# The four half-empty blocks of P turned with 66 columns and copied as 64 partitions; the program's order written as a table of places

## The chip, the cores and the metric

One core of one Trainium2 chip runs the kernel. The metric is device time in microseconds (us) of one execution: 604.06 us before, the median of three runs (603.72 to 604.91). A smaller number is better. The engines are named as in the profile: PE multiplies matrices, PEld is its weight load, DVE, ACT and POOL work on elements, and SP issues most transfers.

## What is computed

Causal attention (batch 4, 12 heads, 448 tokens, head size 64) followed by a two-layer network with squared ReLU (1792 tokens, width 768, hidden width 2048), all in fp32:

```python
attn = softmax(where(causal, q @ k.T / 8, -1e9))        # q, k, v: 4 x 12 x 448 x 64
x = (attn @ v).transpose(0, 2, 1, 3).reshape(1792, 768)
h = maximum(x @ w_in, 0)                                # w_in 768 x 2048
out = (h * h) @ w_out                                   # w_out 2048 x 768
```

## The kernel before

The 48 heads are handled as 24 **pairs** of heads, each in one of two sets of buffers, whose names begin with a or b. In a pair a **chunk** c (0 to 6) is 64 queries of both heads, so 128 partitions. By the causal mask chunk c sees 64(c+1) keys. The steps of a pair are:

- q and k are loaded and turned, on DVE (L403), or for six pairs as rows of 112 tokens on PE (L389).
- PE forms the scores of the chunks (L422). DVE masks each chunk and takes its extreme (L435), ACT takes the exponential and the row sum (L439).
- DVE adds 1e-9 to the seven sums and inverts them (L515, L516). Each chunk of P is then scaled by its inverse, on POOL (L448) or on DVE (L450).
- P is cut into 16 **blocks** (c, kc) of 128 rows by 128 keys, and PE turns them in four **quads** of four (L462). A block is the weight operand, and the identity moves past it. Each quad fills one PSUM bank, and one copy of 128x512 takes it to pt, on ACT (L318) or DVE (L470).
- When all of pt is there, PE multiplies it by v (L482). ACT and DVE split the result into two fp32r halves.

Four blocks, (0,0), (2,1), (4,2) and (6,3), are **half-empty**: only 64 of their 128 keys lie inside the mask. The other half of P was set to zero once, at the start, and is turned like the rest. Before, the list of blocks runs by kc, so the half-empty ones are spread over the quads.

The network's products are made in fp32r as sums of three products (L679 to L681, L1098 to L1100 in the first half). The other half uses a scheme with seven products instead of eight for 2x2 blocks (L860 to L864, L986 to L988). Between these stand the splitting of the weights, loaded as words (L640, L643, L321, L325), and the squares g (L321 on DVE, L325 on POOL).

Every step is an op of a `Plan`. An op has a rank, what it depends on, the buffers that it takes, and one or more ways, each an engine with a cost. Before, `emit` simulated the engines with these costs and took at each step the op that could start first, ties by rank; a table of some hundred amendments shifted ranks. The order that comes out is the order of the instructions in every engine's queue, and each engine works through its queue strictly in that order. The tiles of PSUM (eight banks, `ps`) are handed out in the same pass.

Of the kernel before, what the change touches and what calls it, by code (L numbers as in the profile page):

```python
# [20 lines left out]
class Op:  # L21
    __slots__ = ("rank", "ways", "then", "left", "ready", "take", "drop", "lag", "bias")
# [14 lines left out]
class Plan:  # L37

    LAG = {PE: 0.25, ACT: 0.3, DVE: 0.3, POOL: 0.3, DMA: 0.5, DMA2: 0.5}
    ISSUE = 1.4
    BEGIN, BACKLOG = 1.3, 2.5
    FEW = {PE: 0.0, ACT: 0.5, DVE: 1.0, POOL: 0.0, DMA: 0.0, DMA2: 0.0}
    MANY = {PE: 0.0, ACT: 0.0, DVE: 0.3, POOL: 0.0, DMA: 0.0, DMA2: 0.0}

    def __init__(self):  # L50
        self.ops, self.writer, self.readers = [], {}, {}
        self.pools, self.caps, self.held = {}, {}, {}
        self.bias = self.FEW

# [17 lines left out]
    def op(self, rank, ways, reads=(), writes=(), after=(), take=None, drop=(), clear=(), lag=0.0):  # L72
        o = Op()
        o.rank, o.ways, o.then, o.ready, o.take, o.drop = rank, ways, [], 0.0, take, drop
        o.lag, o.bias = lag, self.bias
# [18 lines left out]
        o.left = len(deps)  # L94
        for d in deps:
            d.then.append(o)
# [3 lines left out]
    def amend(self, table):  # L100
        for first, end, more in table:
            for o in self.ops[first:end]:
                o.rank += more

    def emit(self):
        free = [1.0, 1.9, 3.4, 2.7, 0.7, 0.7]
        ready = [o for o in self.ops if o.left == 0]
        order, port, net = [], 0.0, 0.0
        while ready:
            best = None  # L110
            for o in ready:
                at = o.ready + (self.ISSUE if o.ways[0][0] >= DMA else 0.0)
                if o.take:
                    h, n = o.take[0], len(o.take)
                    if self.held[h.kind] + n > self.caps[h.kind] or len(self.pools[h.pool]) < n:
                        continue
                    at = max(at, sorted(self.pools[h.pool])[n - 1][0])
                at += o.lag
                if o.ways[0][0] >= DMA:
                    at = max(at, net - self.BACKLOG)  # L120

                w = min(
                    (max(free[w[0]], at, port if shared(w) else 0.0) + w[1] + o.bias[w[0]],
                     max(free[w[0]], at, port if shared(w) else 0.0), i, w[0])
                    for i, w in enumerate(o.ways)
                )
                key = (w[1], o.rank)
                if best is None or key < best[0]:
                    best = (key, o, w)
            _, o, (_, start, i, e) = best  # L130
            ready.remove(o)
            free[e] = end = start + o.ways[i][1]
            if shared(o.ways[i]):
                port = max(port, end)
            if e >= DMA:
                net = max(net, start + self.BEGIN) + o.ways[i][3]
                end = max(end, net)
            order.append((start, len(order), o, i))
            for h in o.take:
                entry = min(self.pools[h.pool])  # L140
                self.pools[h.pool].remove(entry)
                h.tile = entry[1:]
                self.held[h.kind] += 1
            for h in o.drop:
                h.drops -= 1
                h.free = max(h.free, end + self.LAG[e])
                if h.drops == 0:
                    self.pools[h.pool].append((h.free,) + h.tile)
                    self.held[h.kind] -= 1
            for t in o.then:  # L150
                same = all(x[0] == e for x in t.ways) and e < DMA
                t.ready = max(t.ready, end + (0.0 if same else self.LAG[e]))
                t.left -= 1
                if t.left == 0:
                    ready.append(t)
        assert len(order) == len(self.ops)
        order.sort(key=lambda x: x[:2])
        for _, _, o, i in order:
            o.ways[i][2]()
        return max(free)  # L160
# [30 lines left out]
def kernel(  # L191
# [47 lines left out]
    TOFF = [P * next(i for i, t in enumerate(TURNED) if t[1] == kc) for kc in range(NK)]  # L239
    NV = 3  # L240
# [10 lines left out]
    class Buffers:  # L251
        def __init__(s, nm, pool):
# [91 lines left out]
    def attention(s, n, at):  # L344
# [109 lines left out]
        def transposed_p(i, at):  # L454

            ps = Hold("ps", "pt")
            blocks = TURNED[4 * i:4 * i + 4]

            def go():
                for n, (c, kc) in enumerate(blocks):  # L460
                    o = QC * (PLACE[c][0] & 1)
                    nc.tensor.transpose(  # L462
                        ps.t[:, n * P:(n + 1) * P],
                        s.p[:, POFF[c] + kc * P:POFF[c] + (kc + 1) * P], ident[:, o:o + P])
            plan.op(at, [(PE, 4 * 0.109, go)], [(nm, "p", c) for c, _ in blocks], [ps],
                    take=ps, clear=[(nm, "pt", i)], lag=spare(1.6))
            t = s.pt[:, 4 * i * P:4 * (i + 1) * P]
            plan.op(at, [
                on_act(512, lambda: t, lambda: ps.t, True),
                (DVE, t_dve(512) + 0.05, lambda: nc.vector.tensor_copy(t, ps.t)),  # L470
            ], [ps], [(nm, "pt", i)], drop=[ps])

        def times_v(av, at):
# [3 lines left out]
            def go():  # L477
                for kc in range(NK):
# [8 lines left out]
                    [(vr, kc) for kc in range(NK)] + [(nm, "pt", i) for i in range(len(TURNED) // 4)], [av], take=av, drop=[vr],  # L487
# [35 lines left out]
        for i in range(len(TURNED) // 4):  # L523
            transposed_p(i, at)
# [675 lines left out]
    plan.bias = plan.MANY  # L1200
# [8 lines left out]
    for gr, u in stages:  # L1209
# [7 lines left out]
    AMENDS = (  # L1217
# [83 lines left out]
```

## Time and profile before

| | before |
|---|---|
| median of three runs | 604.06 us |
| the profiled execution | 606.17 us, of which its span is 604.3 us |
| TensorE's granted clock, mean | 0.999 of full speed |
| PE busy | 587.0 us, 97% of the span |
| weight loads (PEld) | 513.8 us, 85% |
| DVE / ACT / POOL busy | 418.8 / 361.8 / 348.1 us (69 / 60 / 58%) |

Busy time says in which share of the span an engine had something running. The wait view says for whom an engine stood idle. The timeline gives starts, from which the distance between successive instructions is read; a matmul's own duration includes its way through the array, so the distance, not the duration, is what one more of them costs.

### The profile page before, as it was taken

The numbers are of one execution on the slowest core, as the hardware profiler recorded it, in microseconds if no ns is written. First come the engines' busy times: TensorE is split into PE (matmuls) and PEld (weight loads), VectorE is DVE, ScalarE is ACT, GpSimd is POOL, SyncE is SP. The second block draws the span as 40 slices with busy tenths as digits, with TensorE's granted clock in tenths as the row PEclk, the third lists the DMA queues.
The fourth block names the chain that finished last, engine by engine and source line by source line (L and its number), as shares of the span: only waits on it lengthen the run. The fifth ranks groups of instructions, "written<-read, shape, count | busy, mean of one in ns | idle before, by whom it ended". The sixth has DMA issues, their size and how long they took to land.

```text
span 604.3 us, 11456 instructions
## 1 busy us (share of the span) xinstructions
PE 587.0 (97%) x3766; PEld 513.8 (85%) x3766; DVE 418.8 (69%) x951; ACT 361.8 (60%) x889; POOL 348.1 (58%) x460
## 2 busy tenths in 40 slices
PE   3999999999999999999999999999999999999997
PEld 2677777898988998888898889998999899999996
DVE  4997976366985887775677616688782777777454
ACT  3889997665687656577447543367764573752400
POOL 2574673764585844867557754256685566777000
PEclk9999999999999999999999999999999999999999
DMA  9899745979789888987898759869868746771555
GB/s 148 168 204 179 165 103 116 257 232 329 191 208 315 247 238 217 282 232 226 255 242 259 268 189 263 274 188 238 207 152 163 195 116 135 158 177 41 183 92 93
DMA packets 190652, 120.02 MB, mean 199 GB/s; under 512 B 126016, under 2 KB 178560, under 8 KB 190592
## 3 DMA queue, kind: packets, MB, share of 16 engines
q1 hardware_dynamic: 169488, 107.99, 64.8%
q0 software_dynamic: 6912, 9.44, 10.0%
q10 hardware_dynamic: 14192, 1.85, 1.9%
q8 instruction: 30, 0.49, 0.3%
q14 instruction: 30, 0.25, 0.2%
HBM read 80.71 MB, written 38.54 MB: 197 GB/s over the span
## 4 chain that ended last, share of the span: by engine, by line
PE 90%; DMA 4%; ACT 2%; SPq 2%; issue 1%; DVE 0%; ACTq 0%; DVEq 0%
PE ps L1098 7%; PE ps L679 7%; PE ps L1100 6%; PE ps L1099 6%; PE ps L681 6%; PE ps L680 6%; PE ps L482 6%; PE ps L462 6%; PE ps L986 6%; PE ps L988 6%; PE ps L987 6%; PE ps L422 5%; PE ps L860 5%; PE ps L864 5%; PE ps L862 5%; DMA words<-in_moe_w_in_dram 2%
## 5 line engine op out<-in xcount | busy, mean ns | idle before, releaser
L318 ACT ACTIVATE words<-words 128x384 f32<-128x384 f32 (+3 forms) x140 | 79.8, 597 | 27.9 <-DVE words L321 15.3
L448 POOL TENSOR_SCALAR ap<-ap,asm 128x64 f32<-128x64 f32 (+6 forms) x123 | 74.6, 626 | 30.6 <-DVE asm L516 27.7
L435 DVE CUSTOM_DVE_ANT_0 ps<-ps,mask 128x448 f32<-128x448 f32 (+6 forms) x168 | 68.4, 446 | 19.2 <-PE ps L422 12.9
L1098 PE MATMUL ps<-wo,g 128*128 128x384 f32 x224 | 76.8, 343 | 0.0
L1100 PE MATMUL ps<-wo,g 128*128 128x384 f32 x224 | 75.1, 335 | 0.0
L1099 PE MATMUL ps<-wo,g 128*128 128x384 f32 x224 | 75.0, 335 | 0.0
L679 PE MATMUL ps<-x,wi 128*128 128x448 f32 x192 | 74.1, 386 | 0.6 <-ACT aqt L318 0.6
L681 PE MATMUL ps<-x,wi 128*128 128x448 f32 x192 | 70.3, 366 | 0.0
L680 PE MATMUL ps<-x,wi 128*128 128x448 f32 x192 | 70.3, 366 | 0.0
L439 ACT ACTIVATE ap<-ps,mx 128x448 f32<-128x448 f32 (+6 forms) x126 | 59.2, 487 | 15.0 <-DVE mx L435 11.1
L325 POOL TENSOR_TENSOR wi<-words,wi 128x384 fp32r<-128x384 f32 (+1 forms) x44 | 52.6, 1204 | 11.8 <-ACT wi L318 6.6
L860 PE MATMUL ps<-x,wi 128*128 128x448 f32 x156 | 57.3, 367 | 0.3 <-DMA wi<-wi_split 0.3
L318 ACT ACTIVATE r<-ps 128x448 f32<-128x448 f32 x60 | 32.5, 545 | 41.4 <-PE ps L681 17.5
L862 PE MATMUL ps<-x,wi 128*128 128x448 f32 x156 | 57.2, 367 | 0.0
L864 PE MATMUL ps<-x,wi 128*128 128x448 f32 x156 | 57.2, 367 | 0.0
L986 PE MATMUL ps<-g,wi 128*128 128x448 f32 x153 | 56.0, 366 | 0.3 <-DMA wi<-wo_split 0.3
L987 PE MATMUL ps<-g,wi 128*128 128x448 f32 x153 | 56.0, 366 | 0.0
L988 PE MATMUL ps<-g,wi 128*128 128x448 f32 x153 | 56.0, 366 | 0.0
L331 POOL TENSOR_SCALAR wi<-words 128x384 fp32r<-128x384 f32 (+1 forms) x39 | 26.9, 689 | 46.6 <-DVE words L643 23.0
L640 DVE TENSOR_SCALAR words<-words 128x384 int32<-128x384 int32 (+1 forms) x56 | 30.3, 543 | 23.2 <-ACT words L318 23.1
L321 DVE CUSTOM_DVE_ANT_0 words<-words 128x768 uint16<-128x768 uint16 (+1 forms) x56 | 42.3, 755 | 5.8 <-ACT words L318 3.3
L318 ACT ACTIVATE apt<-ps 128x512 f32<-128x512 f32 x65 | 35.6, 611 | 14.5 <-PE ps L462 14.4
(149 smaller groups left out, 1459.9 us busy)
## 6 DMA issues: line engine op xcount, KB each, us to landing
words<-in_moe_w_in_dram SPq DMA_DIRECT2D x24, 512.0 KB, 5.6
words<-in_moe_w_out_dram SPq DMA_DIRECT2D x32, 384.0 KB, 3.7
wo_split<-wo SPq DMA_DIRECT2D x26, 384.0 KB, 4.8
wi<-wo_split SPq DMA_DIRECT2D x24, 384.0 KB, 4.1
wo_whole<-words SPq DMA_DIRECT2D x32, 192.0 KB, 3.9
wi_split<-wi SPq DMA_DIRECT2D x24, 256.0 KB, 4.0
v<-in_v_dram SPq DMA_DIRECT2D x24, 192.0 KB, 4.1
wi_whole<-words SPq DMA_DIRECT2D x18, 256.0 KB, 4.0
```

What stands on the lines that cost most here:

```text
L318: return (ACT, t_act(n, psum, more), lambda: nc.scalar.activation(dst(), src(), func, **kw))
L679: nc.tensor.matmul(o, w[:, 0], x[:, 0], start=c == 0, stop=False)
L680: nc.tensor.matmul(o, w[:, 0], x[:, 1], start=False, stop=False)
L681: nc.tensor.matmul(o, w[:, 1], x[:, 0], start=False, stop=c == NP - 1)
L860: nc.tensor.matmul(o, w.t[:, 0, c], x[:, 0], start=begin and c == 0, stop=False, skip_group_check=True)
L862: nc.tensor.matmul(o, w.t[:, 0, c], x[:, 1], start=False, stop=False, skip_group_check=True)
L986: nc.tensor.matmul(o, w.t[:, 0, d], g.t[:, 0], start=start, stop=False, skip_group_check=True)
L987: nc.tensor.matmul(o, w.t[:, 0, d], g.t[:, 1], start=False, stop=False, skip_group_check=True)
L988: nc.tensor.matmul(o, w.t[:, 1, d], g.t[:, 0], start=False, stop=stop, skip_group_check=True)
L1098: nc.tensor.matmul(res(), g[:, 0], w[:, 0], start=f == 0, stop=False)
L1099: nc.tensor.matmul(res(), g[:, 0], w[:, 1], start=False, stop=False)
L1100: nc.tensor.matmul(res(), g[:, 1], w[:, 0], start=False, stop=f == GF - 1)
```

## The change

The list `QUADS` names the quads by hand. Three have four full blocks each, and the last one collects the four half-empty blocks. In it the weight operand is 66 columns wide (`SLIM`) instead of 128, so the result has 66 partitions instead of 128; the identity that moves keeps its 128 columns. Of the result 64 partitions are copied to pt, in two copies of 64 partitions by 2x128 that wait for the same PSUM bank. The lower 64 partitions of these blocks of pt are set to zero at the start, and of P only two columns per half-empty block. A full quad's copy is one instruction still, of 128x512 or 128x2x256 elements. `emit` no longer plans: it sorts the ops by a table `PLACES` with one number for each op, whose remainder by 3 chooses the way.

```diff
+    QUADS = (
+        ((5, 0), (6, 0), (5, 1), (6, 1)),
+        ((1, 0), (2, 0), (3, 0), (4, 0)),
+        ((3, 1), (4, 1), (5, 2), (6, 2)),
+        tuple((2 * kc, kc) for kc in range(NK)),
+    )
+    SLIM = QC + 2
...
-            for c in range(NQ):
-                if CW[c] < CK[c] * P:
-                    nc.vector.memset(s.p[:, POFF[c] + CW[c]:POFF[c] + CK[c] * P], 0.0)
+            for c, kc in QUADS[-1]:
+                nc.vector.memset(s.p[:, POFF[c] + CW[c]:POFF[c] + kc * P + SLIM], 0.0)
+                nc.vector.memset(s.pt[QC:, TOFF[kc]:TOFF[kc] + P], 0.0)
...
-            blocks = TURNED[4 * i:4 * i + 4]
+            blocks = QUADS[i]
+            slim = i == len(QUADS) - 1
+            m = SLIM if slim else P
...
-                        ps.t[:, n * P:(n + 1) * P],
-                        s.p[:, POFF[c] + kc * P:POFF[c] + (kc + 1) * P], ident[:, o:o + P])
-            plan.op(at, [(PE, 4 * 0.109, go)], [(nm, "p", c) for c, _ in blocks], [ps],
-                    take=ps, clear=[(nm, "pt", i)], lag=spare(1.6))
+                        ps.t[:m, n * P:(n + 1) * P],
+                        s.p[:, POFF[c] + kc * P:POFF[c] + kc * P + m], ident[:, o:o + P])
+            plan.op(at, [(PE, 4 * (0.067 if slim else 0.109), go)], [(nm, "p", c) for c, _ in blocks], [ps],
+                    take=ps, clear=[(nm, "pt", i, h) for h in range(2)] if slim else [(nm, "pt", i)], lag=spare(1.6))
...
+            if slim:
+                for h in range(2):
+                    copied(2 * h, 2 * h + 2, [(nm, "pt", i, h)], slice(0, QC))
+            else:
+                copied(0, 4, [(nm, "pt", i)])
...
-        plan.emit()
+        plan.emit(PLACES)
```

The order moves on all engines. PE has as many rows in its order as before. Its first turned blocks, of the first pair, stand in the same places behind the scores of the first two pairs (`ap` is P of buffer a, `ps` with a number a PSUM bank). Before:

```order
L422 MATMUL ps_120<-bkt,bqt 64x64 x2
L462 MATMUL ps_113<-ident,ap 128x128 x4
L462 MATMUL ps_114<-ident,ap 128x128 x4
L462 MATMUL ps_116<-ident,ap 128x128 x4
L462 MATMUL ps_115<-ident,ap 128x128 x4
L422 MATMUL ps_118<-akt,aqt 64x320 x2
```

And now:

```order
L369 MATMUL ps_124<-bkt,bqt 64x64 x2
L411 MATMUL ps_118<-ident,ap 128x128 x4
L411 MATMUL ps_117<-ident,ap 66x128 x4
L411 MATMUL ps_120<-ident,ap 128x128 x4
L411 MATMUL ps_119<-ident,ap 128x128 x4
L369 MATMUL ps_122<-akt,aqt 64x448 x2
```

One of the four quads is 66 wide, here the second; the scores behind them begin with another chunk, and no row moved past them. On DVE, between the masks of the first pair (`mask`, with the extreme `mx`) and the inverse of its sums (`asm`), the order before is this, behind five other masks of that pair:

```order
L435 ISA ps_116,mx_110<-ps_116,mask 128x192
L435 ISA mx_110 128x1
L435 ISA ps_115,mx_111<-ps_115,mask 128x128
L435 ISA mx_111 128x1
L403 STREAM_TRANSPOSE bkt<-bk 128x448
L403 STREAM_TRANSPOSE bqt<-bq 128x448
L515 TENSOR_SCALAR asm<-asm 128x7
L516 RECIPROCAL asm<-asm 128x7
L403 STREAM_TRANSPOSE akt<-ak 128x448
```

And now, behind three masks of that pair:

```order
L350 STREAM_TRANSPOSE bkt<-bk 128x448
L382 ISA ps_120,mx_112<-ps_120,mask 128x256
L382 ISA mx_112 128x1
L350 STREAM_TRANSPOSE bqt<-bq 128x448
L382 ISA ps_119,mx_113<-ps_119,mask 128x128
L382 ISA mx_113 128x1
L350 STREAM_TRANSPOSE akt<-ak 128x448
L382 ISA ps_120,mx_114<-ps_120,mask 128x192
L382 ISA mx_114 128x1
L382 ISA ps_119,mx_115<-ps_119,mask 128x320
L382 ISA mx_115 128x1
L484 TENSOR_SCALAR asm<-asm 128x7
```

The turning of the second pair's q and k went ahead of three masks, and so did the third pair's k; the inverse of the first pair's sums now stands behind all of these. Later in the program work went from ACT and POOL to DVE. A stretch of DVE's order now, around row 317 of its 1073 (940 before), where a pair's inverse is followed by four of its scalings and by copies to pt:

```order
L484 TENSOR_SCALAR asm<-asm 128x7
L485 RECIPROCAL asm<-asm 128x7
L397 TENSOR_SCALAR ap<-ap,asm 128x320
L397 TENSOR_SCALAR ap<-ap,asm 128x64
L268 TENSOR_TENSOR x_94<-ps_121,x_94 128x448
L397 TENSOR_SCALAR ap<-ap,asm 128x256
L397 TENSOR_SCALAR ap<-ap,asm 128x192
L268 TENSOR_TENSOR g_99<-r_104,g_99 128x448
L268 TENSOR_TENSOR r_105<-r_105 128x448
L432 COPY apt<-ps_124 64x2x128
L268 TENSOR_TENSOR wo<-words,wo 128x384 x2
L432 COPY apt<-ps_120 128x2x256
```

Before, the like place on DVE (around row 309 of 940) held one scaling, and no copy to pt:

```order
L515 TENSOR_SCALAR asm<-asm 128x7
L516 RECIPROCAL asm<-asm 128x7
L321 TENSOR_TENSOR g_94<-r_99,g_94 128x448
L450 TENSOR_SCALAR ap<-ap,asm 128x384
L640 TENSOR_SCALAR words<-words 128x384
L321 ISA words<-words 128x768
L643 SCALAR_TENSOR_TENSOR words<-words 128x384
L1110 COPY acc<-ps_115 128x384
```

Scalings and copies to pt moved from POOL and ACT to DVE there. Counted over the whole order, DVE has 56 more scalings of P (POOL as many fewer), 11 more copies of a full quad and 23 of half-empty blocks. ACT has 35 fewer copies of a full quad and 25 of half-empty blocks. Some 30 two-operand steps of the weights' split and of the squares also went from POOL to DVE. The last stage, behind the last attention pair, has the same steps in the same shape.

## Rows read from the trace of the kernel before

**Rows 1.** Page, parts 1 and 4: busy shares; the chain that ended last.

```profile
PE 587.0 (97%) x3766; PEld 513.8 (85%) x3766; DVE 418.8 (69%) x951; ACT 361.8 (60%) x889; POOL 348.1 (58%) x460
...
PE 90%; DMA 4%; ACT 2%; SPq 2%; issue 1%; DVE 0%; ACTq 0%; DVEq 0%
```

**Rows 2.** Windows of 25 us: busy of each engine, granted clock.

```profile
0.00:25.00 25.00, 13.95 (x135) 9.69 (x136) 16.35 (x65) 13.56 (x45) 9.02 (x26) 1.00 0.84 146
25.00:50.00 25.00, 23.62 (x225) 17.22 (x224) 22.02 (x72) 22.38 (x71) 16.58 (x28) 1.00 1.01 200
50.00:75.00 25.00, 25.00 (x254) 18.47 (x254) 21.51 (x75) 23.64 (x70) 15.53 (x30) 1.00 0.85 174
...
100.00:125.00 25.00, 25.00 (x172) 20.95 (x172) 13.11 (x40) 18.73 (x52) 14.08 (x19) 1.00 0.78 199
```

**Rows 3.** Waits of PE, longest first: total, times, longest.

```profile
PE ps L422 <- DVE aqt L403: 7.3, 2, 6.7
PE ps L422 <- DVE asm L515: 3.2, 1, 3.2
...
PE ps L482 <- DVE apt L470: 0.5, 1, 0.5
```

**Rows 4.** Groups of PE and of weight loads (PEld), shapes apart.

```profile
L462 PE MATMUL ps<-ident,ap 128*128 128x128 f32 x288 | 37.3, 273 | 0.1
...
L462 PE MATMUL ps<-ident,bp 128*128 128x128 f32 x96 | 12.9, 275 | 0.0
...
L389 PE MATMUL ps<-ident,rows 112*128 112x112 f32 x48 | 6.4, 265 | 0.3 <-ACT bp L439 0.3
...
L462 PEld LDWEIGHTS ps<-ident,ap 128*128 128x128 f32 x288 | 33.3, 141 | 2.6 <-issue 0.5
...
L1063 PEld LDWEIGHTS ps<-ident,sb 128*64 128x64 f32 x1 | 0.1, 112 | 0.0
```

**Rows 5.** Timeline of PE in short windows: start, length, count.

```profile
27.45 0.55 PE L482 MATMUL ps<-bpt,v 128*64 128x448 f32 x2
...
27.83 0.44 PE L482 MATMUL ps<-bpt,v 128*64 128x320 f32 x2
...
57.24 0.93 PE L389 MATMUL ps<-ident,rows 112*128 112x112 f32 x8
...
101.55 0.36 PE L680 MATMUL ps<-x,wi 128*128 128x448 f32 x1
101.75 0.37 PE L681 MATMUL ps<-x,wi 128*128 128x448 f32 x1
101.96 1.03 PE L462 MATMUL ps<-ident,bp 128*128 128x128 f32 x8
```

**Rows 6.** Groups of ACT, DVE and POOL, shapes apart.

```profile
L318 ACT ACTIVATE apt<-ps 128x512 f32<-128x512 f32 x65 | 35.6, 611 | 14.5 <-PE ps L462 14.4
L318 ACT ACTIVATE r<-ps 128x448 f32<-128x448 f32 x60 | 32.5, 545 | 41.4 <-PE ps L681 17.5 <-DVE r L558 9.1 <-PE ps L864 9.0
...
L470 DVE COPY apt<-ps 128x512 f32<-128x512 f32 x7 | 4.8, 683 | 10.2 <-PE ps L462 10.2
...
L450 DVE TENSOR_SCALAR ap<-ap,asm 128x384 f32<-128x384 f32 x1 | 0.5, 475 | 0.0
...
L448 POOL TENSOR_SCALAR ap<-ap,asm 128x384 f32<-128x384 f32 x17 | 12.4, 730 | 0.4 <-DVE asm L516 0.4
```

**Rows 7.** Timeline of DVE and PE over the first 17 us.

```profile
1.12 0.33 DVE L263 MEMSET bp<- 128x64 f32 x4
5.50 0.65 DVE L403 STREAM_TRANSPOSE akt<-ak 128x448 f32<-128x448 f32 x1 [4.05 <-DMA ak<-in_k_dram]
...
13.09 0.13 DVE L515 TENSOR_SCALAR asm<-asm 128x7 f32<-128x7 f32 x1
...
13.22 3.10 PE L422 MATMUL ps<-bkt,bqt 64*64 64x320 f32 x28 [3.22 <-DVE asm L515]
16.25 1.99 PE L462 MATMUL ps<-ident,ap 128*128 128x128 f32 x16
```

More of the change, by code (lines that the diff above doesn't have):

```diff
@@ L21 @@
 class Op:
-    __slots__ = ("rank", "ways", "then", "left", "ready", "take", "drop", "lag", "bias")
+    __slots__ = ("rank", "ways", "take", "drop", "deps")
 class Hold:
@@ L37 @@
 class Plan:
[L44 to L48, printed above, removed]
     def __init__(self):
@@ L73, in op @@
         o = Op()
-        o.rank, o.ways, o.then, o.ready, o.take, o.drop = rank, ways, [], 0.0, take, drop
-        o.lag, o.bias = lag, self.bias
+        o.rank, o.ways, o.drop = rank, ways, drop
         o.take = () if take is None else take if isinstance(take, tuple) else (take,)
@@ L93, in op, with emit @@
                 self.readers.setdefault(k, []).append(o)
-        o.left = len(deps)
-        for d in deps:
-            d.then.append(o)
+        o.deps = deps
         self.ops.append(o)
         return o
[L100 to L138, printed above, removed]
+    def emit(self, table):
+        codes = [int(x, 36) for x in table.split()]
+        assert len(codes) == len(self.ops)
+        done = set()
+        for n, (code, o) in enumerate(sorted(zip(codes, self.ops), key=lambda x: x[0])):
+            assert all(d in done for d in o.deps)
             for h in o.take:
@@ L142, in emit @@
                 h.tile = entry[1:]
-                self.held[h.kind] += 1
+            o.ways[code % 3][2]()
             for h in o.drop:
                 h.drops -= 1
-                h.free = max(h.free, end + self.LAG[e])
                 if h.drops == 0:
[L148 to L160, printed above, removed]
+                    self.pools[h.pool].append((n + 1,) + h.tile)
+            done.add(o)
 def t_mm(n, m=128):
@@ L462, in go, with copied, dst, src @@
                     nc.tensor.transpose(
-                        ps.t[:, n * P:(n + 1) * P],
-                        s.p[:, POFF[c] + kc * P:POFF[c] + (kc + 1) * P], ident[:, o:o + P])
-            plan.op(at, [(PE, 4 * 0.109, go)], [(nm, "p", c) for c, _ in blocks], [ps],
-                    take=ps, clear=[(nm, "pt", i)], lag=spare(1.6))
[L467 to L471, printed above, removed]
+                        ps.t[:m, n * P:(n + 1) * P],
+                        s.p[:, POFF[c] + kc * P:POFF[c] + kc * P + m], ident[:, o:o + P])
+            plan.op(at, [(PE, 4 * (0.067 if slim else 0.109), go)], [(nm, "p", c) for c, _ in blocks], [ps],
+                    take=ps, clear=[(nm, "pt", i, h) for h in range(2)] if slim else [(nm, "pt", i)], lag=spare(1.6))
+            def copied(a, b, keys, part=slice(None)):
+                first, gap = (TOFF[kc] // P + c - 2 * kc for c, kc in (blocks[a], blocks[a + (b - a) // 2]))
+                gap -= first
+                w = (b - a) // 2
+                n = w * P * 2
+                def dst():
+                    lead = min(first, gap - w)
+                    t = s.pt[part, (first - lead) * P:(first - lead + 2 * gap) * P]
+                    return t.rearrange("p (u x) -> p u x", u=2)[:, :, lead * P:(lead + w) * P]
+                def src():
+                    return ps.t[part, a * P:b * P].rearrange("p (u x) -> p u x", u=2)
+                plan.op(at, [
+                    on_act(n, dst, src, True),
+                    (DVE, t_dve(n) + 0.05, lambda: nc.vector.tensor_copy(dst(), src())),
+                ], [ps], keys, drop=[ps])
+            if slim:
[3 more added lines that the diff above has]
+                copied(0, 4, [(nm, "pt", i)])
+        KEYS = [(nm, "pt", i) for i in range(len(QUADS) - 1)] + [(nm, "pt", len(QUADS) - 1, h) for h in range(2)]
         def times_v(av, at):
@@ L486, in times_v @@
             plan.op(at, [(PE, 0.2 + 4 * sum((S - kc * P) / 2400 for kc in range(NK)), go)],
-                    [(vr, kc) for kc in range(NK)] + [(nm, "pt", i) for i in range(len(TURNED) // 4)], [av], take=av, drop=[vr],
+                    [(vr, kc) for kc in range(NK)] + KEYS, [av], take=av, drop=[vr],
                     lag=spare(1.0))
@@ L522, in attention @@
         av = Hold("ps", "av")
-        for i in range(len(TURNED) // 4):
+        for i in range(len(QUADS)):
             transposed_p(i, at)
```

131 lines of the change are left out of this document (126 added, 5 removed), and 48 rows, old and new, of the table AMENDS.

## The prediction, made before the changed kernel ran

> **What bounds the kernel now.** I read the page first: PE is busy 97% of the span, and the chain that ended last is PE for 90% of it [rows 1]. The reader should see that no other engine comes near this; DVE, at 69%, is the next. Then the windows, because a mean hides stages: PE is busy 13.95 of the first 25 us and 23.62 of the next, and from 50 us on all 25.00 of 25, at the full granted clock [rows 2]. So in the first 50 us PE can stand idle for a result, and behind them a microsecond less of PE's own work is a microsecond less of the span, as long as the others keep up. The waits of PE agree: the large ones are 7.3 us for the first turned q, and 3.2 us for scores that a line of DVE's early work holds up; what there is besides is 0.5 us and the like, once each [rows 3]. In the windows from 25 to 75 us DVE is busy 22.02 and 21.51 of 25, so it has some 3 us free in each, and from 100 to 125 us it has 12 [rows 2].
>
> **The turned blocks.** There are 384 of them, 288 + 96 [rows 4], and a quarter, 96, becomes 66 wide. What one costs is the distance to the next. Eight in a row last 1.03 us, of which the last takes 0.273 by its own row; (1.03 - 0.27) / 7 = 0.109 us [rows 4, 5]. Now no row has a 66-wide one, so I bound it by neighbours. The upper bound is no gain at all, 0.109. For it speaks the turning of the rows of q and k: its weights are 128 columns wide as well, but 112 columns move, and eight last 0.93 us, so (0.93 - 0.265) / 7 = 0.095 [rows 4, 5], in the ratio of the moving columns, 112 to 128. The change leaves 128 moving columns. The lower bound comes from the fp32 products with v, whose weights are 64 columns wide. Two of them, side by side in the array, start 0.38 us before the next two (27.45 to 27.83) while 448 columns move [rows 5], so 0.19 us for each, 0.42 ns for a moving column. At 128 columns that is 0.055 us. The fp32r product, with one pass and 128-wide weights, starts 0.20 us after the one before it for 448 columns (101.55 to 101.75) [rows 5], 0.45 ns a column, 0.057 at 128, so half of the 0.109 is a rate that the array has. What doubles it, the fp32 operand whatever the weights' width, or the width together with the operand, the rows don't separate. Of the two fp32 rows the one with 64 columns is nearer to 66 than the one with 128, and the last load of a 64-wide block took 112 ns beside 141 for a wide one [rows 4], so the load shrinks too. The changed code counts 0.067 for one of these, beside 0.109 for a full one, and the second figure is what the trace shows. I take 0.067: it lies 0.012 above the lower bound, as it should for a lone product whose load has no neighbour to hide behind.
>
> That saves 0.042 us each. The eight of the first two pairs stand where PE waits anyway, so 88 count: 88 x 0.042 = 3.7 us. At the lower bound it is 88 x 0.054 = 4.8, at the upper one nothing.
>
> By the Trainium skill, page "TensorE: Matmul & The Clock Gate", section "LDWEIGHTS (loading the stationary operand)", a load takes as many ns as its columns divided by 1.2, so 107 ns for 128 and 55 ns for 66. As an estimate from that page the 96 would save 96 x 0.052 = 5.0 us, if the load is what spaces them. The trace is against it: with 128-wide weights the rows of q and k follow each other every 0.095 us [rows 4, 5], less than 107 ns.
>
> **The copies.** Each pair has one instruction more, two of 64x2x128 in place of one of 128x512. On ACT 512 elements take 611 ns and 448 take 545 [rows 6], so 1.03 ns an element and 0.35 us for 256: two are 0.70, 0.09 more than one. Over 24 pairs that is 2.1 us of ACT or DVE, hidden while PE doesn't wait; uncovered, it would hold a product with v by 0.09 us. It goes the other way as well, since both wait for one bank and may run on two engines at once. I count nothing.
>
> **The memsets.** Eight of 128x64 become 8 of 128x2 and 8 of 64x128, on DVE before its first load. Four last 0.33 us now [rows 7]. The eight added ones, twice as wide, are at most 1.3 us by that. DVE then stands idle for 4.05 us until the first k is there [rows 7], which covers it.
>
> **The work that moved to DVE.** 56 scalings by 0.475 us are 27 us (on POOL 0.730 each), 11 full copies by 0.683 are 8 [rows 6], and 23 narrow ones, at 0.683 - 0.26 (the 256 elements less at ACT's 1.03 ns), some 10. With the two-operand steps, 30 at a copy's price, or 20, DVE gains about 65 us, so from 419 to 484, 80% of the span. ACT loses 35 x 0.61 and gains 25 x 0.35, so 13 less. Most of the moved work stands behind 100 us, where DVE has room [rows 2], and the room hides it. Queued behind each such step are masks and sums, and for a mask that comes late the scores' bank stays taken, and PE behind it waits. The waits of that kind that I see cost 0.5 us, one each [rows 3]; I count one more of them, 0.5.
>
> **The start.** PE's second pair of scores starts at 13.22, since q and k of that pair are turned behind the seven masks of the first [rows 7]. With the turning ahead of three masks of 0.5 us or so the scores start up to 1.5 us earlier. But the inverse of the first sums, at 13.09 now [rows 7], comes later by the third pair's k (0.65 us) and what is left, and the first turned blocks, at 16.25, wait for inverse and scaling. PE gains before them and loses at them. I take nothing, plus or minus 1.5.
>
> **The sum.** -3.7 + 0.5 = -3.2 us. The profiled execution took 606.17 us, its span 604.3; it would be 603.0. The median of the runs is 2.1 us below the profiled one, 604.06, so 600.9 us.
>
> **The rivals.**
>
> *The period follows the moving columns.* Then the 66-wide ones still cost 0.109, and the narrow quad saves nothing. The rows of q and k say this plainly; that the 64-wide products take half of it per column, taken singly, speaks against it, but two of them run side by side, which can hide a double price. The time is 604.06 + 0.5, so 604.6. [...]
>
> *The load alone spaces them*, and a 66-wide one gets the lower bound: 604.06 - 4.8 + 0.5 = 599.8. [...]
>
> *DVE is late* (the other side). In the 100 us with the first pairs it is busy up to 22 of 25 us [rows 2], and each scaling or copy put ahead of a mask delays the mask by 0.5 to 0.7 us. If that happens once in each of the first 12 pairs, PE waits 12 x 0.55 = 6.6 us, and the kernel takes 604.06 - 3.7 + 6.6 = 607.0. It decides from seven such waits on (7 x 0.55 = 3.9, more than what is saved). Against it: most of what moved stands later, where DVE has 12 of 25 us free.
>
> **How the numbers follow.** A measurement of this kernel can tell about 0.2% from no change, 1.2 us. My forecast of a part of the gain gets 0.45, no gain on PE 0.27, the full gain 0.10, DVE late 0.18. Faster: 0.42 of the first, all of the third, and 0.06 of the second if the start gives its 1.5 us, so 0.58. Within 0.2%: 0.03 of the first, 0.13 of the second, 0.02 of the last, so 0.18. Slower: 0.08 of the second, where the start loses its 1.5, and 0.16 of the last, so 0.24. The range reaches down to the full gain with a start that gives 1.5, 598.3, and up to where DVE's lateness has eaten the saving and 2 us more, 606.3; I leave out the far half of the last rival. If the forecast holds, 599.5 to 602.5.
>
> **What would show it.** The distance of the 66-wide turned blocks: 0.067 is my forecast, 0.109 the first rival, 0.055 the second. PE's busy time would fall from 587.0 by about the saving, while 25.00 of 25 stays in the windows from 50 us on. PE's waits for DVE's masks, sums and copies behind 50 us, nearly none now, would show the third rival by their number, and the windows would show DVE over 23 of 25 there. In the start, the second pair's scores should stand before 13.22, and the first turned blocks within 1.5 us of 16.25. The prediction is wrong if the distance doesn't change, or if PE has more than 3 us of new waits behind 50 us.

## The result, and the profile after

| | before | changed |
|---|---|---|
| median of 5 runs, same chip | 604.06 us | 609.49 us |
| lowest to highest | 603.71 to 604.91 | 608.69 to 610.07 |
| profiled execution, span | 606.17, 604.3 us | 608.97, 607.2 us |

The changed kernel takes 1.0082 of the time before, 95% interval [1.0071, 1.0093]: some 5.0 us more (0.0082 x 604.06), where 3.2 us less was forecast, and above the range. The profiled execution of before was one of its longer ones, so the two spans differ by 2.9 us only; sizes below are taken from ratios, and the traces say where.

Parts 1 and 4 of the page of after, which answer to [rows 1]:

```profile
PE 587.6 (97%) x3766; PEld 515.1 (85%) x3766; DVE 459.7 (76%) x1080; ACT 345.5 (57%) x871; POOL 286.6 (47%) x381
...
PE 89%; DVE 4%; ACT 3%; issue 2%; POOL 1%; DMA 1%; SPq 0%; POOLq 0%; DVEq 0%; ACTq 0%
```

The first sign is PE's own busy time. It should have fallen from 587.0 by 3.7 us, and stands at 587.6. DVE has risen by 41 us and POOL has lost 61.5, so the work did move. Was PE waiting? Its waits, longest first (total, times, longest), against [rows 3]:

```profile
PE ps L369 <- DVE akt L350: 7.2, 1, 7.2
PE ps L411 <- POOL ap L395: 3.2, 2, 2.6
PE ps L955 <- DVE r L268: 3.1, 2, 1.6
PE ps L369 <- DVE bqt L350: 1.6, 1, 1.6
PE ps L1032 <- DVE sb L268: 0.5, 1, 0.5
```

Two things are new: the wait of the first turned blocks for POOL's scaled P, and two waits for a step r of DVE at L268. The windows say where (against [rows 2]):

```profile
0.00:25.00 25.00, 12.91 (x107) 8.10 (x109) 14.93 (x66) 11.10 (x35) 8.58 (x24) 0.93 0.84 154
25.00:50.00 25.00, 24.67 (x241) 18.49 (x238) 23.13 (x81) 23.69 (x77) 14.66 (x24) 1.00 0.88 201
50.00:75.00 25.00, 25.00 (x253) 18.85 (x255) 23.53 (x80) 23.65 (x75) 12.30 (x23) 1.00 0.64 133
...
225.00:250.00 25.00, 25.00 (x167) 22.49 (x166) 23.64 (x55) 12.34 (x33) 8.97 (x12) 1.00 0.79 204
425.00:450.00 25.00, 23.55 (x117) 21.50 (x116) 17.13 (x25) 17.25 (x37) 15.49 (x20) 1.00 0.70 148
525.00:550.00 25.00, 23.37 (x116) 21.29 (x115) 17.27 (x25) 10.73 (x22) 17.09 (x21) 1.00 0.65 155
```

The reader should see that the losses are not where DVE is fullest. DVE is busy 23.5 of 25 us from 50 to 75 and 23.6 from 225 to 250, and PE is at 25.00 in both. PE loses 1.5 and 1.6 us in two windows of the last stage in which DVE is busy 17 of 25, and about a microsecond in the first window.

**The turned blocks.** One full quad and one 66-wide quad, 1.1 us apart in PE's timeline (start, length), and then the groups of the two widths' weight loads:

```profile
33.38 0.60 PE L411 MATMUL ps<-ident,ap 128*128 128x128 f32 x4
...
34.46 0.60 PE L411 MATMUL ps<-ident,ap 128*66 128x128 f32 x4
```

```profile
L411 PEld LDWEIGHTS ps<-ident,ap 128*128 128x128 f32 x216 | 26.5, 144 | 5.4 <-POOL ap L395 3.0
...
L411 PEld LDWEIGHTS ps<-ident,ap 128*66 128x66 f32 x72 | 7.9, 115 | 2.2 <-POOL ap L395 0.9 <-issue 0.2
```

Both quads last 0.60 us. Less the last block's own 0.28 (the mean of the 66-wide ones is 280 ns), (0.60 - 0.28) / 3 is 0.107 us. From start to start, over the 72 distances between two 66-wide blocks, the median is 0.109, as between two full ones. The load did get shorter, 144 to 115 ns, and the distance did not follow it.

**The start.** ACT's first rows before and after, then the row of PE that answers to 16.25 in [rows 7], with the inverse and the scaling that it waits for, and last the window of after in which those blocks run:

```profile
5.97 1.28 ACT L439 ACT_TABLE_LOAD   x1 [5.97 <-DMA bq<-in_q_dram]
9.37 0.63 ACT L439 ACTIVATE ap<-ps,mx 128x448 f32<-128x448 f32 x1 [2.11 <-DVE mx L435]
```

```profile
10.73 1.28 ACT L386 ACT_TABLE_LOAD   x1 [10.73 <-DVE mx L382]
12.03 0.58 ACT L386 ACTIVATE ap<-ps,mx 128x384 f32<-128x384 f32 x1
...
15.68 0.17 DVE L484 TENSOR_SCALAR asm<-asm 128x7 f32<-128x7 f32 x1 [0.68 <-ACT ap L386]
...
16.30 3.36 POOL L395 TENSOR_SCALAR ap<-ap,asm 128x192 f32<-128x192 f32 x7 [13.29 <-DVE asm L485]
...
17.96 0.66 PE L411 MATMUL ps<-ident,ap 128*128 128x128 f32 x4 [2.58 <-POOL ap L395]
19.27 2.77 PE L411 MATMUL ps<-ident,ap 128*66 128x128 f32 x12 [0.65 <-POOL ap L395]
```

```profile
20.00:22.00 2.00, 2.00 (x14) 1.67 (x12) 1.80 (x6) 1.89 (x6) 0.55 (x2) 0.50 0.71 132
```

Before, ACT loaded its table while it had nothing to do, and stood ready. Now the load itself waits for DVE's mask, and the first exponential starts at 12.03 in place of 9.37. The inverse stands at 15.68 (13.09 before), the first turned blocks at 17.96 (16.25), and the first product of the networks at 33.74 (30.20). There is a second loss in it. Twelve turned blocks last 2.77 us, where before 16 of them lasted 1.99 [rows 7]: from start to start they are 0.213 apart, twice 0.109, and the window in which they run shows the granted clock (the column after POOL's) at 0.50, the 1.2 GHz of its two levels. PE had stood idle for 2.58 and 0.65 us ahead of them. Part of the lag is only work in another order: at the 300th such product the lag is down to 1.9 us, at the 1320th 1.3. (The trace of before is itself a late one: that of before_exp, below, in which only two exponentials changed places, is 1.6 us ahead of it from the 100th product to the 1320th.) A small loss stands ahead of all this: DVE now turns q first, at 5.98, where it turned k at 5.50, and PE's first scores begin at 7.21 in place of 6.73.

**The last stage.** DVE, POOL and PE around the first of the two losses:

```profile
430.17 1.19 POOL L721 TENSOR_SCALAR words<-words 128x384 f32<-128x384 f32 x1
...
430.62 3.17 DVE L268 TENSOR_TENSOR g<-f,g 128x448 fp32r<-128x448 f32 x1
...
431.04 1.31 POOL L272 TENSOR_TENSOR wi<-words,wi 128x384 fp32r<-128x384 f32 x1
...
432.02 1.27 POOL L272 TENSOR_TENSOR wi<-f,wi 128x384 fp32r<-128x384 f32 x1
...
433.71 0.61 DVE L268 TENSOR_TENSOR r<-ps,f 128x448 f32<-128x448 f32 x1
...
434.38 0.47 PE L955 MATMUL ps<-g,wi 128*128 128x448 f32 x1 [1.45 <-DVE r L268]
```

and around the second:

```profile
534.30 2.70 DVE L268 TENSOR_TENSOR f<-f,r 128x448 f32<-128x448 f32 x1
...
534.67 1.83 POOL L272 TENSOR_TENSOR r<-r,f 128x448 f32<-128x448 f32 x1
...
537.46 0.61 DVE L268 TENSOR_TENSOR r<-ps,f 128x448 f32<-128x448 f32 x1
...
538.12 0.48 PE L955 MATMUL ps<-g,w 128*128 128x448 f32 x1 [1.63 <-DVE r L268]
```

A two-operand step of DVE that takes 0.61 us elsewhere in these rows takes 3.17 and 2.70 beside POOL's two-operand steps, and in both places it ends half a microsecond after the last of POOL's (433.79 to 433.30, 537.00 to 536.50): its own work comes when POOL's is over. The step r<-ps,f, which empties a bank for PE, is queued behind it. The Trainium skill has this as a rule, page "SBUF — State Buffer", section "Who interferes with whom": a DVE instruction with two SBUF inputs and a GpSimd instruction that reads SBUF exclude each other, and one of them blocks fully. The trace agrees, and adds that DVE can stay blocked over two of POOL's two-operand steps in a row. Which of the two goes first these records leave open: at the first place a step of POOL that reads SBUF (430.17) was already running when DVE's began, at the second DVE's record begins 0.37 us ahead of POOL's.

### The profile page after: what moved, and what is told of

Same layout as the page of the kernel before. It is cut to its first block, busy times and chain, and to the rows that moved or that the text cites. A ratio compares the mean times of both kernels' runs of the same rounds, so it can differ in the third digit from the quotient of the medians.

```text
span 607.2 us, 11446 instructions
## 1 busy us (share of the span) xinstructions
PE 587.6 (97%) x3766; PEld 515.1 (85%) x3766; DVE 459.7 (76%) x1080; ACT 345.5 (57%) x871; POOL 286.6 (47%) x381
## 4 chain that ended last, share of the span: by engine, by line
PE 89%; DVE 4%; ACT 3%; issue 2%; POOL 1%; DMA 1%; SPq 0%; POOLq 0%; DVEq 0%; ACTq 0%
PE ps L451 7%; PE ps L648 7%; PE ps L411 7%; PE ps L1067 7%; PE ps L1069 6%; PE ps L1068 6%; PE ps L649 6%; PE ps L650 6%; PE ps L369 6%; PE ps L955 5%; PE ps L956 5%; PE ps L957 5%; PE ps L833 5%; PE ps L829 5%; PE ps L831 5%
## 5 line engine op out<-in xcount | busy, mean ns | idle before, releaser
L265 ACT ACTIVATE words<-words 128x384 f32<-128x384 f32 (+3 forms) x132 | 76.1, 593 | 34.8 <-DVE words L268 11.0
L382 DVE CUSTOM_DVE_ANT_0 ps<-ps,mask 128x128 f32<-128x128 f32 (+6 forms) x168 | 68.2, 441 | 13.7 <-PE ps L369 9.2
L386 ACT ACTIVATE ap<-ps,mx 128x64 f32<-128x64 f32 (+6 forms) x126 | 58.5, 473 | 19.4 <-DVE mx L382 18.8
L272 POOL TENSOR_TENSOR wi<-words,wi 128x384 fp32r<-128x384 f32 (+1 forms) x48 | 57.5, 1214 | 23.5 <-ACT wi L265 18.5
L395 POOL TENSOR_SCALAR ap<-ap,asm 128x384 f32<-128x384 f32 (+6 forms) x71 | 41.6, 601 | 54.3 <-DVE asm L485 23.2
L955 PE MATMUL ps<-g,wi 128*128 128x448 f32 x159 | 58.2, 366 | 1.4 <-DVE r L268 1.4
L957 PE MATMUL ps<-g,wi 128*128 128x448 f32 x159 | 58.1, 365 | 0.0
L956 PE MATMUL ps<-g,wi 128*128 128x448 f32 x159 | 58.1, 365 | 0.0
L268 DVE TENSOR_TENSOR g<-r,g 128x448 fp32r<-128x448 f32 x55 | 43.2, 789 | 8.1 <-ACT g L265 4.5
L411 PE MATMUL ps<-ident,ap 128*128 128x128 f32 (+1 forms) x288 | 41.6, 279 | 3.2 <-POOL ap L395 3.2
L1067 PEld LDWEIGHTS ps<-wo,g 128*128 128x128 f32 x224 | 42.1, 188 | 0.7
```

Of the source, the lines that this page charges most:

```text
L265: return (ACT, t_act(n, psum, more), lambda: nc.scalar.activation(dst(), src(), func, **kw))
L955: nc.tensor.matmul(o, w.t[:, 0, d], g.t[:, 0], start=start, stop=False, skip_group_check=True)
L956: nc.tensor.matmul(o, w.t[:, 0, d], g.t[:, 1], start=False, stop=False, skip_group_check=True)
L957: nc.tensor.matmul(o, w.t[:, 1, d], g.t[:, 0], start=False, stop=stop, skip_group_check=True)
L1067: nc.tensor.matmul(res(), g[:, 0], w[:, 0], start=f == 0, stop=False)
```

## The experiments

Theory going in: the 66-wide blocks save nothing, and the 5 us are lost through the order alone, in the start (through the table load) and in two places of the last stage (through DVE's held steps). Rival: the new blocks, their width, their copies and their zeros cost something of their own. Each ratio is to the kernel before on the same chip.

**after_exp.** The changed kernel with the first pair's exponential of 448 columns again ahead of that of 384. A row of ops is dealt out over its own places; nothing else moves.

```diff
+ROWS_OF = ((17, 19, 21),)
...
+        for row in ROWS_OF:
+            at = sorted(i for i, x in enumerate(line) if x[1] in row)
+            way = {x[1]: x[0] for x in line}
+            for i, k in zip(at, row):
+                line[i] = (way[k], k)
```

> The changed kernel with one swap in its order: on ACT the exponential of the 448-wide chunk of the first pair comes first again, ahead of those of 384 and 64. Theory (the load of ACT's function table, 1.28 us, stands at 10.73 in the changed kernel because it waits together with the first exponential, and at 5.97, while ACT has nothing to do, before): the table load goes back to about 6, the first exponential starts at about 9.8 instead of 12.03, the first turned blocks at about 16 to 16.5 instead of 17.96, and the kernel takes 1.3 to 2 us less than the changed one, 607.5 to 608.2. Rival (the start is late because the masks and turnings changed places on DVE, the table load is a bystander): the first turned blocks stay at 17.5 or later and the time at 609.0 to 609.5.

```profile
6.07 1.28 ACT L403 ACT_TABLE_LOAD   x1 [6.07 <-DMA bq<-in_q_dram]
9.96 0.63 ACT L403 ACTIVATE ap<-ps,mx 128x448 f32<-128x448 f32 x1 [2.60 <-DVE mx L399]
```

608.82 us, 1.0069 [1.0057, 1.0082]. The load is back where ACT stands idle, and the first turned blocks start at 16.65 in place of 17.96. The time falls by 0.0013 x 604, 0.8 us, less than I had expected, and the interval overlaps that of the changed kernel, so by itself this gain is not clear of the noise (after_both says more). In its trace 12 of the first turned blocks' distances are about twice 0.109 here too, so the part of the start that goes to the slower rate stays; the granted clock reads 1.00 from 16 to 22 us in this trace.

**after_apart.** The changed kernel with the two places of the last stage mended: at the first, r<-ps,f (op 2578) goes ahead of the held step (2517); at the second, POOL's r<-r,f (3111) runs on DVE.

```diff
+ROWS_OF = ((2575, 2576, 2577, 2578, 2517),)
+FLIP = {3111: -1}
...
+            code += FLIP.get(k, 0)
```

> The changed kernel with its order altered at the two places of the last stage where PE waits for DVE (434.4 and 538.1): at the first, the sum r<-ps,f for which PE waits goes ahead of the product g<-f,g that lasted 3.2 us; at the second, the sum r<-r,f goes from POOL to DVE. Theory (a two-operand step of DVE stands still while POOL has two-operand steps of its own, and PE waits for what is queued behind it): both waits, 1.5 and 1.6 us, go, and the kernel takes 2.5 to 3.5 us less than the changed one, 606 to 607. Rival (these waits make up for time that would be lost behind them anyway): the waits go, but new ones come up in the last 170 us, and the time stays at 608.5 to 609.5.

DVE at the first place, then at the second:

```profile
430.55 0.61 DVE L285 TENSOR_TENSOR r<-ps,f 128x448 f32<-128x448 f32 x1
431.09 2.65 DVE L285 TENSOR_TENSOR g<-f,g 128x448 fp32r<-128x448 f32 x1
...
532.53 0.62 DVE L285 TENSOR_TENSOR f<-f,r 128x448 f32<-128x448 f32 x1
```

606.00 us, 1.0020 [1.0008, 1.0031]: 3.7 us less than the changed kernel (0.0062 x 604), and both waits of L955 are gone from PE's list. At the first place the held step is still held, 2.65 us, but nothing that PE needs is behind it. At the second, the same step beside the same work takes 0.62 once POOL's two-operand step is taken from beside it: the hold is shown to be POOL's.

**after_both.** Both of these edits together.

> The changed kernel with both of these alterations. If they are independent the gains add up, to 4 to 5 us, so 604.5 to 605.5, the time of the kernel before within 0.2%. If the start's delay is made up for later, less than 3.5 us, 606 or more.

604.15 us, 0.9995 [0.9985, 1.0006]: the time of before, with the 66-wide blocks, their copies and zeros all in place. Together the two edits take 5.3 us off the changed kernel (0.0087 x 604), where 0.8 and 3.7 make 4.5; on top of after_apart the swap of exponentials takes 1.5, and these two intervals do not overlap. No loss is left over for the rival, though a small one could hide behind what this order gains elsewhere (see the sum below).

**after_wide.** The changed kernel with 128 columns again in the half-empty blocks, and the zeros of P for them.

```diff
-            m = SLIM if slim else P
+            m = P
```

> The changed kernel with 128 columns in place of 66 in the four half-empty blocks; the copies of 64 partitions and the order stay. Theory (a turned block costs what its 128 moving columns cost, whatever the width of the weights): 0.109 us from block to block as with 66 columns, and the same time, 609.0 to 610.0. Rival (66 columns save something that the distances don't show, in the loads or where a group begins): up to 3.7 us more, 611 to 613.

610.01 us, 1.0088 [1.0071, 1.0106], beside 1.0082 for 66 columns. The width makes no difference that these runs can tell; all distances have a median of 0.109 us.

**before_exp.** The kernel before with its two first exponentials changed about, 384 first: does the table load come late there too?

```diff
+        at = sorted(n for n, x in enumerate(order) if x[2] in (self.ops[17], self.ops[19]))
+        order[at[0]], order[at[1]] = order[at[1]], order[at[0]]
```

> The kernel before with one swap: on ACT the exponential of the 384-wide chunk of the first pair comes ahead of that of the 448-wide one, as in the changed kernel. Theory (the table load waits with whichever exponential comes first, when that one waits for two engines): if the load again carries a wait, it goes from 5.97 to about 9.4, the first exponential starts 1.3 us later, and the kernel takes up to 1.3 us more, 605.0 to 606.0; if the 384-wide chunk's exponential waits for DVE alone here, the load stays at 6 and the time at 604.0 to 604.8, and then it is not the swap by itself that moved the load but what that exponential waits for. Rival (the load is a bystander): the load moves and the time doesn't.

604.12 us, 0.9990 [0.9980, 0.9999], and the load stayed at 6.08. So it isn't the chunk. The first two rows below are ACT's order in the changed kernel, the other two in before_exp (the names in brackets are the semaphores waited for):

```
L386 ACT_TABLE_LOAD [waits DVE_49]
L386 ACTIVATE ap,asm<-ps_118,mx_110 128x384 [waits PE_49]
L441 ACT_TABLE_LOAD
L441 ACTIVATE ap,asm<-ps_114,mx_106 128x384 [waits DVE_49]
```

In the changed kernel this exponential has two waits, for DVE and for PE, and one of them stands on the load; here it has one, which it carries itself. The reason that I had first, that 384 is ahead, was too coarse.

**after_96.** What sets the distance? The changed kernel with 96 columns of identity moving through the 66-wide blocks, and 96 rows. It leaves out the last 32 queries of the half-empty blocks.

```diff
-                        ps.t[:m, n * P:(n + 1) * P],
+                        ps.t[:m, n * P:n * P + t],
...
+            t = 3 * P // 4 if slim else P
```

> The changed kernel with 96 of the 128 rows of each half-empty block turned, by an identity of 96 x 96, so that 96 columns move past weights of 66 columns; it leaves out the last 32 queries of these blocks. Theory (the distance follows the moving columns): 0.082 us from block to block, 96 / 128 of 0.109, while 66 wide weights with 128 moving columns took 0.109. Rival (a fixed time for a turned block): 0.109.

PE's timeline, a full quad, and then a 96-column one:

```profile
34.05 0.60 PE L412 MATMUL ps<-ident,ap 128*128 128x128 f32 x4
35.20 0.49 PE L412 MATMUL ps<-ident,ap 96*66 96x96 f32 x4
```

The length falls from 0.60 to 0.49 us, and the median distance between two such blocks to 0.082. With 128, 112 and 96 columns moving the distances are 0.109, 0.096 and 0.082: 0.85 ns a column each time, whatever the weights' width. (Rows went from 128 to 96 as well; with 112 and 128 they also go together in q and k, so these runs don't part columns from rows. Only the columns of the weights are shown to do nothing.) Its one run took 608.25 us.

**before_packed, after_packed.** If a block costs its moving columns, the way to gain is fewer blocks. Here two half-empty blocks lie side by side in P and are turned as one of 128 columns, so 48 blocks fewer: once in the kernel before with its planner, once in after_both. Chunk 4 has its keys in another order for it, so its scores are written in two pieces.

```diff
+    ROW = (2, 0, 6, 4, 1, 3, 5)
+    POFF = [sum(CW[d] for d in ROW[:ROW.index(c)]) for c in range(NQ)]
...
+                if slim:
+                    for n, c in enumerate((2, 6)):
+                        o = QC * (PLACE[c][0] & 1)
+                        first = POFF[c] + CW[c] - QC
+                        nc.tensor.transpose(ps.t[:, n * P:(n + 1) * P], s.p[:, first:first + P], ident[:, o:o + P])
+                    return
```

> The order's planner, amendments and engines of the kernel before, with P laid out so that two half-empty blocks lie side by side, (2,1) with (0,0) and (6,3) with (4,2): one turned block of 128 columns in place of two. It needs the keys of chunk 4 with the last 64 ahead of the first 256, so its scores take two products per head instead of one. 48 turned blocks fewer. Theory (a turned block costs 0.109 whatever its width, and PE has nothing to spare behind 50 us): 48 x 0.109 = 5.2 us less of PE's work, and a time of 599 to 600.5, the planner's order being made for other work. Rival (the time isn't PE's work but the order): 603 or more.

> The changed kernel with both alterations of its order, and with two half-empty blocks turned as one in place of four of 66 columns. Theory: 5.2 us less of PE's work than with both alterations alone (604.2), so 598.5 to 600. Rival (an order made for other durations loses it again in waits): 602 or more, with new waits of PE behind 50 us.

before_packed: 606.37 us, 1.0029 [1.0013, 1.0045], a miss. PE's busy time fell to 585.5 us, but the planner's new order brought waits that neither kernel had:

```profile
PE ps L896 <- DMA wi<-wi_split: 1.7, 1, 1.7
PE ps L1022 <- DMA w<-wo_split: 1.4, 1, 1.4
PE ps L900 <- DVE wi L328: 1.2, 1, 1.2
```

after_packed: 602.29 us, 0.9953 [0.9941, 0.9965], faster than both kernels, but by about half of what I expected of it against after_both, 2.5 us of 5.2, and its time lies in the rival's range, though PE has only one new wait behind 50 us, of 0.3. Summed over its trace, PE's waits left out, the distances between turned blocks fall from 37.0 us (320 of them, in after_both) to 30.8 (272), 6.2 us, and those between products of scores rise from 37.8 (648) to 41.1 (744), 3.3 us. Both sums mix the packing with the rate at the start. In after_both eleven of the first turned blocks' distances are near 0.213, in after_packed none is. Instead the second and third pairs' scores take longer there; these are their rows in after_packed, and then the third pair's in after_both, whose second pair took 1.75 us (last section):

```profile
12.04 3.29 PE L388 MATMUL ps<-bkt,bqt 64*64 64x256 f32 x32 [1.59 <-DVE bqt L367]
19.48 3.06 PE L388 MATMUL ps<-akt,aqt 64*64 64x448 f32 x32 [0.19 <-DVE aqt L367]
```

```profile
20.48 2.06 PE L386 MATMUL ps<-akt,aqt 64*64 64x448 f32 x28
```

Behind 26 us the distances between turned blocks fall by 5.0 us and those between products of scores rise by 0.8. So the packing itself brings about 4.4 us (5.2 less 0.8) in these traces, and the start takes 1.5 of it back (2.5 for the scores, less 1.0 for the blocks), in one execution of each. That makes 2.9; the spans of the two traces differ by 2.0, so 0.9 us stays unplaced.

**after_pack1.** after_both with only two of the four half-empty blocks put together, those that need no split scores: 24 blocks fewer.

```diff
+    ROW = (2, 0, 1, 3, 4, 5, 6)
...
+                    if slim and c == 0:
+                        continue
```

> The changed kernel with both alterations of its order, and with (2,1) and (0,0), which now lie side by side in P, turned as one block of 128 columns; (4,2) and (6,3) stay at 66 columns, and the scores stay whole. 24 turned blocks fewer. Theory: 24 x 0.109 = 2.6 us less than with both alterations alone, 601 to 602. Rival (the order made for other durations loses it in waits): 603.5 or more.

604.24 us, 1.0002 [0.9988, 1.0017], a miss. The distances between turned blocks fall by 3.1 us, and it is given back in pieces. The largest is the same products of scores at another rate: those of the second and third pairs take 3.14 and 2.68 us in its trace, 2.0 us more than the 1.75 and 2.06 in after_both.

```profile
12.13 3.14 PE L389 MATMUL ps<-bkt,bqt 64*64 64x320 f32 x28 [1.65 <-DVE bqt L370]
...
19.89 2.68 PE L389 MATMUL ps<-akt,aqt 64*64 64x448 f32 x28
```

The scores behind 26 us take 0.7 us more, and two new waits for ACT's copies to pt 0.7 in all. Its runs scatter from 603.6 to 607.2.

**before_slim.** The other way about: the 66-wide quads in the kernel before, with its planner in place of the table, and both copies by one engine.

> The planner and amendments of the kernel before with the new quads, 66 columns in the half-empty ones and their two copies of 64 partitions, done one behind the other by one engine; the planner's costs are as before. Theory (the blocks and copies neither cost nor save; the table of places is what costs): 604 to 606, and 0.109 us between the 66-wide blocks. Rival (the new quads themselves cost, because the first one needs the chunks that are scaled last, and because of the copies): 607 or more, with PE waiting for ACT's or DVE's copies.

609.21 us, 1.0074 [1.0062, 1.0087], a miss of 3 to 5 us. The distances are 0.109 here too, and the start is that of before, but PE has waits of the same kind as in before_packed:

```profile
PE ps L885 <- DMA wi<-wi_split: 1.7, 1, 1.7
PE ps L889 <- DVE wi L328: 1.2, 1, 1.2
PE ps L1011 <- DMA w<-wo_split: 1.2, 1, 1.2
```

The quads are enough to make the planner write another order, and this one costs about as much as the table's. before_packed has nearly the same three waits and takes 2.7 us less (1.0029 against 1.0074), which is what the packing gave in the table's order too (2.5).

**after_start.** The changed kernel with before's order of the first pair's masks and exponentials, and three loads moved back with them.

```diff
+ROWS_OF = ((16, 18, 20, 17, 19, 21, 22, 23, 25, 27, 29, 24, 26, 28, 30, 59, 60, 68, 31, 105),)
+BEHIND = ((150, 60), (146, 60), (145, 60))
```

> The changed kernel with the first pair's seven masks on DVE and seven exponentials on ACT in the order of the kernel before, and the turning of the second pair's q and k behind the masks again; three loads of the fourth pair's k move behind these. Theory (of the start's delay the table load is the greater part): the gain is that of the exponentials' swap alone (0.7 us) and up to 0.8 us more, 607.5 to 609. Rival (the interleaving of masks and turnings costs as much as the load): 606.5 or less.

607.53 us, 1.0049 [1.0036, 1.0062]: 2.0 us less than the changed kernel, 1.2 of them beyond the exponential's 0.8. The first turned blocks stand at 16.38. So the start costs some 2 us in all when it is mended alone; this interval lies clear of the changed kernel's. (The split into 0.8 and 1.2 is as rough as the 0.8.)

## Why the prediction was wrong

**The turned blocks, the step that failed first.** "I take 0.067" was wrong: the distance is 0.109, and the saving of 3.7 us is nothing. That is the first rival, to which I gave 0.27. The row that settled it was in my hands: rows of q and k, 128 columns wide in the weights, 0.095 with 112 moving [rows 4, 5]. I let two arguments outweigh it. One was that a 64-wide product is "nearer" to 66, though its 0.19 us came from two that run side by side. In the trace of before these two start 0.007 us apart, so each has the whole 0.376 us to the next for its 448 columns, 0.84 ns a column: read so, this row speaks for the first rival as well. The other was the changed code's own 0.067, a number in a table and no row of the trace. The page "TensorE: Matmul & The Clock Gate" of the Trainium skill bears on both rivals. Its section "LDWEIGHTS (loading the stationary operand)" gives a load's time by its columns; as an estimate from it the distance would be near 55 ns (66 / 1.2) if the load alone set it, which the section does not say. The runs are against that, 0.109 at either width. The section "Back-to-back issue gap" of the same page of the Trainium skill gives the gap of an isolated product by its moving columns, and says that in a stream of loads and products both set the spacing. Here the distance follows the moving columns in proportion, 0.85 ns each, and not the weights' columns.

**DVE late: a wait counted, and mis-sized.** I counted +0.5 for work queued ahead on DVE. There are two such waits, 1.45 and 1.63 us, and taking them away gave 3.7 us. The third rival had the sign and looked in the wrong place: masks in the first 100 us, by DVE's load. From 50 to 425 us PE stood at 25.00 in every window, with DVE as full as 23.6. What I left out is that the price of a step isn't its mean: I priced moved two-operand steps at a copy's 0.68 us, and beside POOL's two-operand steps one takes 3.17. DVE has 16 two-operand steps of over 1.2 us now, 26.3 us together, and had 11 with 16.8 before; behind two of the 16 stood a step r<-ps,f for which PE waited. DVE's total had less to do with it: it rose by 41 us, not by the 65 that I had added up.

**The start.** "I take nothing, plus or minus 1.5." It cost 0.8 us for the table load, and some 2 us with the order of masks. In the trace of the changed kernel 11 distances between turned blocks had 0.104 too much, 1.1 us; how much of that belongs to the order isn't shown. I had read that the inverse would come later, by 0.65 and what was left; it came 2.6 later, 1.28 of which a table load that I had not looked at at all, since in before it was hidden. PE's second scores came at 12.12, ahead of 13.22, as forecast.

**The copies and the memsets** cost nothing, as forecast. The eight added memsets ended at 3.47 us, ahead of DVE's first turning at 5.98, and after_both, with all of them in, takes the time of before.

**The sum with what was measured.** 604.06 + 0 for the blocks + 3.7 for the two places + 0.8 for the load makes 608.6, and with the 2.0 of the whole start 609.8; 609.49 was measured, 609.0 by the ratio. (The upper end of the forecast's range, 606.3, is 0.2 more than its own terms, 604.06 and 2, make.) after_both has the time of before although it keeps about 1.2 us of the start's loss, so something gives as much back. The traces put it in the last stage: from the 1320th of the networks' products to the last one after_both takes 194.2 us and before 1.6 more, 195.7 (before_exp 196.3). There PE in before has two waits for weights that a DMA brings, and in after_both neither:

```profile
PE ps L860 <- DMA wi<-wi_split: 0.3, 1, 0.3
...
PE ps L986 <- DMA wi<-wo_split: 0.3, 1, 0.3
```

The two products that waited start 0.67 and 0.63 us behind the ones ahead of them, where 0.20 is usual, so these two cost 0.9 of the 1.6 us. The prediction had PE at 25.00 in every window from 50 us on, but [rows 2] shows two windows of that stretch, and before reads 24.70 from 400 to 425 and 24.74 from 450 to 475. The rest of the 1.6 us stays open.

## What to carry to other kernels

Before pricing a narrower operand, look which size the distance between two like instructions follows, in rows that differ in one size only; one run with that size alone changed settles it. When an order is rewritten, read three things in it ahead of any mean: what the first instruction of each function on ACT waits for, which two-operand steps of DVE now lie beside two-operand steps of POOL, and which step that empties a bank for PE is queued behind them. The order alone moves this kernel by some 5 us (after_both against the changed kernel; before_slim, with the new quads in it, by 4.5), more than any edit of the work did, so an edit should be timed in an order that is otherwise unchanged.

## What the runs showed that I had not expected

The table load of 1.28 us takes over one of the waits of the first function behind it where that one has two: at 10.73 in place of 5.97, released by DVE's mask.

PE's rate at the start decides over a microsecond, and not by the order alone. Most of the first pair's turned blocks stood 0.213 us apart in the traces of the changed kernel, after_wide, after_exp, after_apart, after_both and before_packed, and 0.109 in those of the kernel before and of after_packed, one execution each. The second pair's 28 products of scores took 3.10 us before [rows 7], 3.26 in the changed kernel and 1.75 in after_both, by these rows of PE's timeline (the changed kernel, then after_both):

```profile
12.12 3.26 PE L369 MATMUL ps<-bkt,bqt 64*64 64x320 f32 x28 [1.65 <-DVE bqt L350]
```

```profile
12.06 1.75 PE L386 MATMUL ps<-bkt,bqt 64*64 64x320 f32 x28 [1.65 <-DVE bqt L367]
```

The same instructions behind the same 1.65 us of idle time ran at either rate, so the order alone does not decide it. The granted clock of short windows doesn't tell all of it either: from 20 to 22 us it is 0.50 in the changed kernel and 1.00 in after_wide, with distances of 0.213 in both, and from 12 to 14 us it is 1.00 in the changed kernel and in after_both, whose scores ran there at the two rates. So what sets the rate there stays open.
